# A fused attention and feed-forward kernel: matmuls of 128x128 issued as two of 128x64, some waits left out, the first loads in parts

## The chip, the cores and the metric

The kernel runs on one core of a Trainium2 chip, alone. The metric is the device time of one execution in microseconds (us), taken as the median of several runs. The engines in what follows are PE (TensorE, the matmuls; PEld is its weight loads), DVE (VectorE), ACT (ScalarE), POOL (GpSimd) and SP (SyncE, which issues most of the transfers).

## The reference

Two stages follow each other: an attention whose scores below the row's maximum less `tau` are dropped, and a feed-forward block with ELU. There are 8 sequences of 8 heads, 576 positions and 64 elements, and 4608 tokens of 512 with 2048 hidden units. Everything is computed in f32; the two weight matrices arrive in f64.

```python
scores = scale * np.matmul(q, k.transpose(0, 1, 3, 2))
thresh = np.max(scores, axis=-1, keepdims=True) - tau
scores = np.where(scores >= thresh, scores, -1000000000.0)
...
attn = np.exp(scores - max)
attn = attn / (np.sum(attn, axis=-1, keepdims=True) + 1e-09)
attn_out = np.matmul(attn, v)                  # (8, 8, 576, 64)
x = attn_out.transpose(0, 2, 1, 3).reshape(4608, 512)
h = x @ w_in                                   # (4608, 2048)
g = np.where(h > 0.0, h, np.exp(np.minimum(h, 0.0)) - 1.0)
return g @ w_out                               # (4608, 512)
```

## The kernel before

**Attention.** Heads are taken in 32 pairs, four for a sequence. For a pair the scores come in blocks of 128 queries; head 0 lies in partitions 0 to 63 and head 1 in 64 to 127. A score matmul (`scores`, L494, in the first sequence; `wide_scores`, L769, and the tails at L816 in the others) has 64 rows and 64 columns of weights, so that four of them fill the array. DVE takes the maximum (L518, L776), POOL the threshold (L522, L782), ACT the exponential (L528, L786), DVE drops what lies below the threshold and sums the rest (L538, L790), POOL or ACT divides by the sum (L429, L502), and the block is turned. The first blocks are turned on PE (L555) and copied out of PSUM; the later ones are turned by DVE in squares of 32 (L641), sent to DRAM (L675) and fetched back as `wTa` and `wTb` (L685). The values matmuls follow: `values` (L708 for the 64 tail positions, L713 for the 512 others) in the first sequence, and L821 and L829 later. L713 and L829 hold 64 columns of weights (one head's V), one head in the upper and one in the lower half of the output.

**Feed-forward.** A few chunks are computed plainly: `ffn1` (L888), `ffn1_block` (L916) and `ffn2_plain` (L956), with 128x128 weights. All the others go by seven products of half-size blocks in place of eight: `first_product` (L1447) for x @ w_in, the second round (L1587) for g @ w_out, and in the last stage, when no attention is left, a deeper split of the second (`deep_product`, L1961, 128 columns, and `plain_product`, L2023). Each of these matmuls has 128 rows and 128 columns of weights and 256 or 128 columns that stream through. ACT, DVE and POOL make the sums of the products and the ELU around them.

**The order.** Up to about the ninth pair the order of work is written out by hand: `EARLY` lists some 1270 jobs, each with the engine that does it after a colon, or the PSUM bank after an @. `job(...)` declares what a job needs. Jobs such as `ld.q.0.0` load, `first.k.0.0` turns a piece of the first sequence on PE, `sc.0`, `max`, `exp`, `th`, `mask` and `norm` are the steps of one score block, `half.x` is half a plain feed-forward job, and `idle17` is a run of 17 transposes of the identity, which keep PE going while nothing is loaded. Behind `EARLY` a planner inside the kernel lays the feed-forward jobs between the attention of each pair, by costs and due times, and the deep stage ends the kernel.

**Waits.** The framework derives an instruction's waits from the tiles that it touches. PSUM banks of the wide score tile are handled by the kernel: `on_banks` (called by `watch` and directly) keeps for each bank who touched it and declares every instruction of another engine on these banks as needed.

Of the kernel before, what the change touches and what calls it, by code (L numbers as in the profile page):

```python
# [15 lines left out]
ALU = mybir.AluOpType  # L16
# [4 lines left out]
    "9:3.0": 0.61, "9:fetch0": -3.6, "9:turn4": 2.44, "e:139.1": 0.46, "e:140.2": -0.49, "e:176.2": 1.07,  # L21
    "e:203p0": 1.03, "e:30.2": 0.35, "e:73p0": 1.88, "e:75p0": 1.3, "e:77.2": -1.81, "e:78.1": -3.94, "e:9b":
    -2.29, "e:e30": -0.75,
# [37 lines left out]
ld.tail.1.0 ld.k.0.0:act ld.k.0.1 ld.tau.0.0:act idle17@f0 ld.q.0.0 ld.k.1.1 ld.k.1.0 lw.0 lw.1 first.t.k.0@f0  # L61
ld.k.2.0 tau copy.k.0 first.k.0.0@f2 ld.k.2.1 idle4@f0 prep.k.0.0 ld.k.3.0 first.q.0.0@f0 first.q.1.0@f2 ld.k.3.1
prep.q.0.0 first.t.k.1@f1 sc.0 copy.k.1:dve ld.tail.0.0 lw.2 first.t.k.2@f0 max.0.0 copy.k.2 prep.q.1.0 first.q.2.0@f0
idle7@t max.0.1 exp.0.0 th.0.0 lw.3 first.k.1.0@f2 th.0.1 exp.0.1 mask.0.0 prep.q.2.0 prep.k.1.0 mask.0.1 idle5@f0
first.t.k.3@f1 shift.0 ld.vd.3.0 sc.1 su.0:act copy.k.3:dve sign.0 ld.q.1.0 shift.1 rec.0 rest.0 ld.q.2.0 norm.0.0
first.q.3.0@f0 max.1.0 ld.vd.0.1 prep.q.3.0 first.k.2.0@f0 max.1.1 ld.v.1.1 exp.1.0 th.1.0 rest.1:pool first.t.q.0@f2
ld.q.3.0 part.0.0@t exp.1.1 mask.1.0 th.1.1 first.k.3.0@f1 add.0 prep.k.2.0 mask.1.1 copy.q.0 first.t.q.1@f0 ld.v.0.0
su.1:act sc.2 end.0 norm.0.1:act shift.2 prep.k.3.0 rec.1 part.0.1@f2 norm.1.1 max.2.0 sign.1 idle21@f1 max.2.1
ld.v.0.1 exp.2.0 th.2.0 rest.2:pool ld.vd.0.0 exp.2.1 mask.2.0 th.2.1 add.1 put.0.0 lw.4 mask.2.1 sign.2 rest.3
norm.1.0 sc.3 end.1 ld.v.1.0 su.2:act copy.q.1 put.0.1 add.2 part.0.2@t turn.0 lw.5 max.3.0 part.1.0@f1 put.0.2  # L70
landed.0 ld.vd.2.1 first.q.0.1@f0 max.3.1 exp.3.0 ld.v.3.1 first.q.1.1@f2 th.3.0 rec.2 part.1.1@t th.3.1 exp.3.1
ld.v.2.1 mask.3.0 norm.2.0 ld.vd.1.1 prep.q.0.1 mask.3.1 put.1.1 ld.vd.1.0 part.1.2@f0 turn.1 put.1.0 shift.3 sc.4
end.2 add.3 sign.3 ld.vd.2.0 put.1.2 landed.1 prep.q.1.1 su.3 val.0.block.0@t max.4.0 lw.6 rec.3 max.4.1 exp.4.0
th.4.0 norm.2.1 first.q.2.1@f0 exp.4.1 mask.4.0 part.2.0@f1 th.4.1 norm.3.0 idle7@f2 ld.vd.3.1 norm.3.1:act mask.4.1
ld.v.2.0 put.2.0 end.3 sc.5 su.4:act out.0.block.0 rest.4 shift.4 lw.7 shift.5 sign.4 add.4 ld.v.3.0 part.2.1@t
max.5.0 prep.q.2.1 part.2.2@f1 turn.2 val.1.block.0@f2 max.5.1 exp.5.0 th.5.0 rec.4 th.5.1 exp.5.1 mask.5.0 norm.4.0
part.3.0@f0 put.2.2 put.2.1 landed.2 mask.5.1 part.3.1@f1 norm.4.1 put.3.0 part.3.2@t turn.3 end.4 out.1.block.0
rest.5:pool sc.6 su.5:act put.3.1 sign.5 lw.8 add.5 val.2.block.0@f0 max.6.0 put.3.2 landed.3 rest.6 max.6.1 shift.6
exp.6.0 th.6.0 part.4.0@t rec.5 th.6.1 exp.6.1 mask.6.0 first.q.3.1@f1 add.6 part.4.1@f2 put.4.0 mask.6.1 prep.q.3.1
part.4.2@t turn.4 sign.6 end.5 sc.7 put.4.1 put.4.2:dve landed.4 lw.9 end.6 norm.5.1:act val.3.block.0@t max.7.0  # L80
out.2.block.0 lw.10 norm.5.0:act su.6 max.7.1 th.7.0 exp.7.0 part.5.0@f0 out.3.block.0:dve th.7.1 exp.7.1 mask.7.0
rest.7:pool part.5.1@t part.5.2@f1 turn.5 val.0.block.1@f2 rec.6 mask.7.1 norm.6.1 norm.6.0:act put.5.0 shift.8
rest.8:pool put.5.2 sc.8 su.7 put.5.1 landed.5 rec.7 shift.7 sign.8 add.7 val.1.block.1@t norm.7.0:act max.8.0 max.8.1
exp.8.0 th.8.0 norm.7.1 part.7.0@f0 out.0.block.1:dve out.1.block.1 mask.8.0 exp.8.1 part.6.0@t th.8.1 add.8
part.7.1@f1 put.7.0 mask.8.1 part.6.1@f2 sign.7 part.7.2@f0 turn.7 su.8 sc.9 put.7.1 end.7 rest.9 end.8 lw.11 put.6.1
half.0@f1 shift.9 load.k.4 put.6.0 rec.8 max.9.0 add.9 norm.8.1:act put.7.2:dve landed.7 exp.9.0 max.9.1 part.6.2@t
turn.6 val.3.block.1@f0 th.9.0 norm.8.0:act mask.9.0 th.9.1 lw.12 rest.10:pool exp.9.1 shift.10 sc.10 out.3.block.1
sign.9 add.10 sign.10 part.8.0@f0 put.6.2:dve mask.9.1 landed.6 max.10.0 part.8.1@t su.9:act part.8.2@f2 turn.8 end.9
half.1 exp.10.0 th.10.0 rec.9 put.8.0 put.8.2 lw.13 put.8.1 mask.10.0 norm.9.0 landed.8 end.10 norm.9.1 su.10:act
first.t.q.3@f2 first.t.q.2@f0 sc.11 copy.q.2 copy.q.3 shift.11 rest.11 lw.14 rec.10 val.2.block.1@t fexp.0.0.0  # L90
norm.10.0 max.11.0 max.11.1 exp.11.0 th.11.0 fmin.0.0.0 part.10.0@f0 out.2.block.1:dve exp.11.1 mask.11.0 th.11.1
part.9.0@t add.11 put.10.0 part.9.1@f2 mask.11.1 sign.11 part.10.1@f0 turn.10 shift.12 sc.12 put.10.1 landed.10 end.11
rest.12 shift.13 sign.12 lw.15 add.12 half.4@f0 max.12.0 su.11:act put.9.0 max.12.1 exp.12.0 th.12.0 rec.11 end.12
th.12.1 rest.13 part.9.2@t turn.9 half.5 mask.12.0 exp.12.1 lw.16 add.13 load.q.4 put.9.2 put.9.1 landed.9 mask.12.1
sign.13 sc.13 elu.0.0.0 norm.11.1 su.12 val.0.1@t rec.12 max.13.0 norm.12.0:act norm.12.1 end.13 exp.13.0 th.13.0
fexp.0.1.0 mask.13.0 norm.11.0:act fmin.0.1.0 turn.12 su.13:act rest.14 in.0.0:pool sc.14 rest.15 in.0.1:pool rec.13
send.12 part.11.0@f1 max.14.0 in.0.2:pool half.8@f2 max.14.1 in.1.0:pool exp.14.0 elu.0.1.0 th.14.0 th.14.1 lw.17
out.0.1 put.11.0 shift.15 part.11.1@f0 shift.14 exp.14.1 part.11.2@t turn.11 half.2@f1 add.14 mask.14.0 sign.14
put.11.1 mask.14.1 landed.12 add.15 norm.13.0:act end.14 sc.15 put.11.2:dve landed.11 lw.18 part.13.0@f0 max.15.0
half.3 su.14 max.15.1 exp.15.0 th.15.0 rec.14 sign.15 th.15.1 mask.15.0 exp.15.1 part.13.1@t turn.13 shift.16 sc.16  # L100
rest.16:pool end.15 put.13.0 prep.q.4 add.16 half.9 put.13.1 landed.13 sign.16 mask.15.1 load.q.5 norm.14.1:act
in.1.1:pool max.16.0 su.15:act in.1.2:pool val.1.1@t shift.17 exp.16.0 prep.k.4 th.16.0 fexp.0.0.1 insend.0
in.2.0:pool norm.14.0:act mask.16.0 lw.19 rest.18:pool fmin.0.0.1:act end.16 rest.17 rec.15 shift.18 su.16:act lw.20
sc.17 add.17 out.1.1 rec.16 elu.0.0.1 norm.15.1:act part.14.0@t max.17.1 fexp.0.0.2 norm.15.0 half.6@f0 put.14.0
max.17.0 norm.16.0 fmin.0.0.2:act turn.15 exp.17.0 in.2.1:pool part.14.1@t exp.17.1 th.17.0 part.14.2@f1 turn.14
th.17.1 half.7 send.15 sign.17 add.18 mask.17.0 put.14.2 mask.17.1 in.2.2:pool elu.0.0.2 part.16.0@f1 su.17:act
sign.18 end.17 sc.18 put.16.0 rec.17 end.18 lw.21 norm.17.0:act half.10@f1 max.18.0 put.14.1 landed.14 max.18.1
landed.15 exp.18.0 th.18.0 rest.19:pool in.3.0 lw.22 exp.18.1 half.11 th.18.1 mask.18.0 in.3.1:pool mask.18.1 sc.19
su.18 fexp.0.0.3 in.3.2 rec.18 shift.19 norm.18.0 norm.18.1:act half.14@f2 max.19.0 fexp.0.1.1 scale.4:act turn.18
exp.19.0 th.19.0 rest.20:pool fmin.0.0.3:act part.16.1@t turn.16 half.15 add.19 send.18 put.16.1 landed.16 mask.19.0  # L110
sign.19 in.4.0 fmin.0.1.1:act su.19:act end.19 val.2.1@t fexp.0.1.3 shift.21 lw.23 rest.22 shift.20 rec.19 elu.0.1.1
rest.21 norm.19.0 fmin.0.1.3:act elu.0.0.3 in.4.1:pool norm.17.1:act elu.0.1.3 landed.18 add.21 in.4.2 part.17.0@f0
load.k.5 part.19.0@f1 prep.q.5 put.17.0 part.17.1@f2 add.20 put.19.0 half.18@f0 sign.20 end.20 shift.22 lw.24 out.2.1
put.17.1 sign.21 part.19.1@t turn.19 in.5.0 add.22 part.17.2@f1 turn.17 half.12@f2 put.19.1 landed.19 end.21 put.17.2
landed.17 in.5.1 in.5.2:pool val.3.1@t shift.23 insend.5 sign.23 insend.4 rest.23 lw.25 sign.22 add.23 copy.k.4:act
end.22 prep.k.5 rest.24:pool lw.26 out.3.1 t tail.4 half.19 bmax.4.4.0 insend.2 shift.24 bexp.4.4.0 bth.4.4 add.24
# [60 lines left out]
def kernel(  # L177
# [281 lines left out]
    WBUFS = 3  # L459
    e_both, e_next = att.tile([P, 2, 2, HALF], FP32, name="e", bufs=1), [0]  # L460

    def e_slot():
        e_next[0] ^= 1
        return e_both[:, e_next[0]]

# [1666 lines left out]
```

## Time and profile before

| what | value |
|---|---|
| median of 3 runs (lowest to highest) | 1264.27 us (1262.33 to 1265.05) |
| profiled execution: its time | 1262.88 us |
| profiled execution: its span | 1261.1 us |
| instructions in the span | 24668 |
| DMA | 277.84 MB, 220 GB/s over the span |
| PE records of L1447, L1587, L1961 and L2023 | 1792, 1344, 476, 176 |
| PE records of L829 and L713 (128x64 already) | 896, 192 |

Lines such as L1447 are those of the kernel before. In a group of matmuls `128*128 128x256 f32 x8` reads: weights of 128 rows and 128 columns, a moving operand of 128 partitions by 256 elements, 8 records. An f32 matmul of the program is two records, each with its weight load, while a transpose is one. Records of PE overlap: one of 256 columns lasts about 380 ns in the list, and the next starts long before it ends. So the time that a matmul costs is the distance between starts, and a mean length or a busy share doesn't tell it.

### The profile page before, as it was taken

The numbers are of one execution on the slowest core, as the hardware profiler recorded it, in microseconds if no ns is written. First come the engines' busy times: TensorE is split into PE (matmuls) and PEld (weight loads), VectorE is DVE, ScalarE is ACT, GpSimd is POOL, SyncE is SP. The second block draws the span as 40 slices with busy tenths as digits, with TensorE's granted clock in tenths as the row PEclk, the third lists the DMA queues.
The fourth block names the chain that finished last, engine by engine and source line by source line (L and its number), as shares of the span: only waits on it lengthen the run. The fifth ranks groups of instructions, "written<-read, shape, count | busy, mean of one in ns | idle before, by whom it ended". The sixth has DMA issues, their size and how long they took to land.

```text
span 1261.1 us, 24668 instructions
## 1 busy us (share of the span) xinstructions
PE 1245.4 (99%) x8187; PEld 970.9 (77%) x8187; DVE 1068.6 (85%) x2322; ACT 584.7 (46%) x1276; POOL 788.6 (63%) x1147
## 2 busy tenths in 40 slices
PE   8999999999999999999999999999999999999998
PEld 5776576477777777777788777777777778899998
DVE  6998989898889979898989888988989885777876
ACT  7987755453444435252625353444535260434130
POOL 5775545586576747674767657674757473675554
PEclk9999999999999999999999999999999999999999
DMA  9568898898989898999889898989889876434433
GB/s 225 147 180 240 226 260 244 240 306 213 254 212 262 233 244 223 260 245 237 241 225 268 218 268 202 269 221 251 215 255 248 237 215 219 166 133 150 143 107 112
DMA packets 332880, 277.84 MB, mean 220 GB/s; under 512 B 201296, under 2 KB 288336, under 8 KB 332752
## 3 DMA queue, kind: packets, MB, share of 16 engines
q1 hardware_dynamic: 331760, 275.73, 78.8%
q8 instruction: 65, 1.06, 0.3%
q10 hardware_dynamic: 992, 0.53, 0.1%
q14 instruction: 63, 0.52, 0.1%
HBM read 178.85 MB, written 97.32 MB: 219 GB/s over the span
## 4 chain that ended last, share of the span: by engine, by line
PE 82%; DVE 3%; issue 1%; ACT 0%; DMA 0%; SPq 0%; POOL 0%; DVEq 0%; ACTq 0%
PE f L1447 30%; PE f L1587 23%; PE sc L829 9%; PE sc L769 8%; PE f L1961 4%; PE f L2023 3%; PE sc L821 1%; PE f L888 1%; PE sc L816 1%; DVE mx L776 1%; PE f L956 1%; DVE x L641 1%; DVE e L790 0%; DVE w_one L790 0%; DMA there<-x 0%
## 5 line engine op out<-in xcount | busy, mean ns | idle before, releaser
L776 DVE TENSOR_REDUCE mx<-sc 128x1 f32<-128x576 f32 x252 | 180.2, 746 | 37.8 <-PE sc L769 32.3
L782 POOL TENSOR_SCALAR th<-mx,ntau 128x2 f32<-128x2 f32 (+1 forms) x140 | 46.0, 329 | 187.1 <-DVE mx L776 186.9
L786 ACT ACTIVATE w_one<-sc,mx 128x576 f32<-128x576 f32 x140 | 100.8, 741 | 132.7 <-DVE mx L776 113.3
L790 DVE SCALAR_TENSOR_TENSOR w_one<-sc,th,w_one 128x576 f32<-128x576 f32 x140 | 110.0, 813 | 20.4 <-ACT w_one L786 20.2
L769 PE MATMUL sc<-kT,qT 64*64 64x256 f32 (+5 forms) x1792 | 124.2, 410 | 2.4 <-DVE su L546 0.5
L1447 PE MATMUL f<-xt,sw 128*128 128x256 f32 x512 | 123.8, 384 | 0.6 <-ACT xt L432 0.5
L786 ACT ACTIVATE e<-sc,mx 128x576 f32<-128x576 f32 x112 | 82.8, 743 | 86.6 <-DVE mx L776 85.0
L1447 PE MATMUL f<-x,w_in_sb 128*128 128x256 f32 x512 | 122.8, 382 | 0.0
L1447 PE MATMUL f<-xt,w_in_sb 128*128 128x256 f32 x512 | 121.2, 379 | 0.5 <-DVE xt L1056 0.5
L769 PEld LDWEIGHTS sc<-kT,qT 64*64 64x64 f32 x1792 | 80.7, 132 | 48.3 <-issue 18.2
L502 POOL TENSOR_SCALAR w_one<-w_one,rs 128x576 f32<-128x576 f32 x115 | 89.4, 788 | 38.7 <-DVE rs L552 38.7
L641 DVE STREAM_TRANSPOSE x<-w_one 128x512 f32<-128x512 f32 (+1 forms) x140 | 99.9, 744 | 14.2 <-POOL w_one L502 9.5
L1447 PEld LDWEIGHTS f<-xt,sw 128*128 128x128 f32 x512 | 94.1, 190 | 21.1 <-issue 5.8
L1447 PEld LDWEIGHTS f<-x,w_in_sb 128*128 128x128 f32 x512 | 96.2, 190 | 16.2 <-ACT g L1508 3.6
L1447 PEld LDWEIGHTS f<-xt,w_in_sb 128*128 128x128 f32 x512 | 97.2, 190 | 14.0 <-ACT e L786 0.8
L790 DVE SCALAR_TENSOR_TENSOR e<-sc,th,e 128x576 f32<-128x576 f32 x112 | 87.7, 808 | 8.3 <-ACT e L786 7.9
L1587 PE MATMUL f<-w_out_sb,g 128*128 128x256 f32 x384 | 92.0, 382 | 0.0
L1587 PE MATMUL f<-w_out_sb,s 128*128 128x256 f32 x384 | 91.9, 382 | 0.0
L1587 PE MATMUL f<-t,s 128*128 128x256 f32 x384 | 90.7, 379 | 0.0
L1587 PEld LDWEIGHTS f<-w_out_sb,g 128*128 128x128 f32 x384 | 72.0, 190 | 13.1 <-issue 3.8
L1587 PEld LDWEIGHTS f<-w_out_sb,s 128*128 128x128 f32 x384 | 71.9, 190 | 12.7 <-issue 3.2
L502 POOL TENSOR_SCALAR e<-e,rs 128x576 f32<-128x576 f32 x92 | 67.8, 742 | 20.8 <-DVE rs L552 18.3
(344 smaller groups left out, 2894.1 us busy)
## 6 DMA issues: line engine op xcount, KB each, us to landing
there<-x SPq DMA_DIRECT2D x452, 144.0 KB, 3.8
wTb<-there SPq DMA_DIRECT2D x58, 576.0 KB, 6.4
wTa<-there SPq DMA_DIRECT2D x55, 576.0 KB, 4.7
sw<-win_sums SPq DMA_DIRECT2D x62, 384.0 KB, 4.3
t<-wout_sums SPq DMA_DIRECT2D x45, 512.0 KB, 5.3
there<-x SPq DMA_DIRECT2D x112, 80.0 KB, 1.9
wTb<-there SPq DMA_DIRECT2D x56, 160.0 KB, 3.6
wst<-in_moe_w_in_dram SPq DMA_DIRECT2D x16, 512.0 KB, 4.8
```

The source lines that it names most:

```text
L502: nc.gpsimd.tensor_scalar(wv, wv, st["rs"][:, h : h + 1], 1.0, ALU.mult, ALU.mult)
L641: nc.vector.transpose(x[:, :, c0 : c0 + nc_], src.rearrange("p (c g n) -> p g c n", c=nc_, n=T))
L769: on_banks(nc.tensor.matmul(oy, qT[r, i * P + y * D : i * P + (y + 1) * D], kT[r, k0 : k0 + n], start=True, stop=True, skip_group_check=Tr ...
L776: on_banks(nc.vector.tensor_reduce(st["mx"][:, h : h + 1], st["sc", h], axis=AX.XY if i == NC else AX.X, op=ALU.max, negate=True), st["sc" ...
L782: nc.gpsimd.tensor_scalar(st["th"][:, cs], st["mx"][:, cs], -1.0, ntau, ALU.mult, ALU.add)
L786: on_banks(nc.scalar.activation(st["e", h], st["sc", h], AF.Exp, bias=st["mx"][:, h : h + 1]), st["sc", h])
L790: on_banks(nc.vector.scalar_tensor_tensor(st["e", h], st["sc", h], st["th"][:, h : h + 1], st["e", h], ALU.is_ge, ALU.mult, accum_out=st[" ...
L829: on_banks(nc.tensor.matmul(o, vm[:, h, c], parts[part][:, g0:g1, h * (NC + 1) + c], start=False, stop=(c == NC - 1), skip_group_check=Tru ...
L1447: nc.tensor.matmul(loc["banks"][place], left[:, j], right[:, j], start=(begins and j == 0), stop=(j == 1), skip_group_check=True)
L1587: nc.tensor.matmul(place(m), lhs, rhs, start=(begins and v == 0), stop=(v == RU - 1), skip_group_check=True)
L1961: nc.tensor.matmul(loc["x"][place][:, :P], left[:, v], right[:, v], start=(begins and v == 0), stop=(v == 1), skip_group_check=True)
L2023: nc.tensor.matmul(loc[c][:, :HM], lefts(g, r, c, m)[:, v], rights(r, m)[:, v], start=(v == 0), stop=(v == RU - 1), skip_group_check=True)
```

## The change

- A new helper, `by_columns`, issues a matmul of 128 output rows as two of 64, with the two halves of the weights' columns, the same moving operand and the two halves of the output's partitions. It takes the place of one `nc.tensor.matmul` in `values` (L708), `first_product` (L1447), the second round (L1587), `deep_product` (L1961) and `plain_product` (L2023). `ffn1`, `ffn1_block`, `ffn2_plain` and the transposes stay as they were. The program has 6142 matmuls for 4225.
- `on_banks` passes its list through the new `followed`, which drops a need that another one in the list, or an earlier instruction of the engine, already implies. `exp_of` declares that it needn't wait for the exponential which last wrote its slot.
- The loads of the first 128 queries and of the K tails are made in two parts: heads 0 and 1, then 2 to 7. Each turning job needs only the part that it reads.
- The threshold job may be done by ACT as well as POOL.
- `EARLY` is another order: some 350 of 1270 jobs stand a few places elsewhere, 24 on another engine.

```diff
     def exp_of(pr, i, h):
...
-        on_banks(nc.scalar.activation(e, o, AF.Exp, bias=st["mx"][:, h : h + 1]), o)
+        made = nc.scalar.activation(e, o, AF.Exp, bias=st["mx"][:, h : h + 1])
+        if slot_exps[e_next[0]]:
+            tc.declare_no_dep(made.ins, slot_exps[e_next[0]].name, reason="its mask lies between")
+        slot_exps[e_next[0]] = made.ins
+        on_banks(made, o)
...
-        watch(nc.tensor.matmul(pv[:, :n], vd, wT[:, :, NC], start=True, stop=False, skip_group_check=True), pv[:, :n])
+        by_columns(pv[:, :n], vd, wT[:, :, NC], watch, start=True, stop=False)
...
+    serials, known = {}, {}
+
+    def followed(ins, engine, needed):
+        have = known.setdefault(engine, {})
+        kept_ = []
+        for x in needed:
+            e, n, _ = serials[x.name]
+            if n > have.get(e, -1) and not any(serials[y.name][2].get(e, -1) >= n for y in needed if y is not x and serials[y.name][0] != e):
+                kept_.append(x)
+        for x in kept_:
+            e, n, seen = serials[x.name]
+            for z, m in {**seen, e: n}.items():
+                have[z] = max(have.get(z, -1), m)
+        serials[ins.name] = engine, len(serials), dict(have)
+        return kept_
...
+        needed = followed(ins, engine, needed)
...
+    def by_columns(o, left, right, note=None, **how):
+        n = o.shape[0]
+        for y in range(0, n, D):
+            oy = o[y : y + D] if n > D else o
+            made = nc.tensor.matmul(oy, left[:, y : y + D] if n > D else left, right, skip_group_check=True, **how)
+            if note:
+                note(made, oy)
...
             if what == "q":
-                return w_out_sb[:, NPAIR + z].rearrange("p (h d) -> p h d", d=D), q[0, :, z * P : (z + 1) * P].rearrange("h p d -> p h d")
+                hs = (slice(0, H), slice(0, 2), slice(2, H))[h]
+                return w_out_sb[:, NPAIR + z].rearrange("p (h d) -> p h d", d=D)[:, hs], q[0, hs, z * P : (z + 1) * P].rearrange("h p d -> p h d")
             if what == "tail":
-                return first_tails("qk"[z]), (q, k)[z][0, :, MAIN:].rearrange("h t d -> t h d")
+                hs = (slice(0, H), slice(0, 2), slice(2, H))[h]
+                return first_tails("qk"[z])[:, hs], (q, k)[z][0, hs, MAIN:].rearrange("h t d -> t h d")
...
-                job(("th", n, h), "pool", lambda e, pr=pr, i=i, h=h: bound_of(pr, i, h), ("max", n, h), "tau")
+                job(("th", n, h), "pool|act", lambda e, pr=pr, i=i, h=h: bound_of(pr, i, h, e), ("max", n, h), "tau")
...
                 for j in range(2):
-                    nc.tensor.matmul(loc["banks"][place], left[:, j], right[:, j], start=(begins and j == 0), stop=(j == 1),
-                                     skip_group_check=True)
+                    by_columns(loc["banks"][place], left[:, j], right[:, j], start=(begins and j == 0), stop=(j == 1))
...
-                        nc.tensor.matmul(place(m), lhs, rhs, start=(begins and v == 0), stop=(v == RU - 1),
-                                         skip_group_check=True)
+                        by_columns(place(m), lhs, rhs, start=(begins and v == 0), stop=(v == RU - 1))
...
-                    nc.tensor.matmul(loc["x"][place][:, :P], left[:, v], right[:, v], start=(begins and v == 0), stop=(v == 1),
-                                     skip_group_check=True)
+                    by_columns(loc["x"][place][:, :P], left[:, v], right[:, v], start=(begins and v == 0), stop=(v == 1))
...
-                    nc.tensor.matmul(loc[c][:, :HM], lefts(g, r, c, m)[:, v], rights(r, m)[:, v], start=(v == 0), stop=(v == RU - 1),
-                                     skip_group_check=True)
+                    by_columns(loc[c][:, :HM], lefts(g, r, c, m)[:, v], rights(r, m)[:, v], start=(v == 0), stop=(v == RU - 1))
...
-ld.tail.1.0 ld.k.0.0:act ld.k.0.1 ld.tau.0.0:act idle17@f0 ld.q.0.0 ld.k.1.1 ld.k.1.0 lw.0 lw.1 first.t.k.0@f0
+ld.tail.1.1 ld.k.0.0:act ld.k.0.1 ld.q.0.1:act ld.tau.0.0 ld.tail.1.2:act idle17@f2 ld.q.0.2 ld.k.1.0:act ld.k.3.1
```

More of the change, by code (lines that the diff above doesn't have):

```diff
@@ L86 @@
[L86 to L95, printed above, removed]
@@ L101 @@
[L101 to L105, printed above, removed]
```

229 lines of the change are left out of this document (126 added, 103 removed).

## The prediction

> **What bounds the kernel now.** I read the page first, its busy table and the chain that ended last:
>
> ```profile
> span 1261.1 us, 24668 instructions
> PE 1245.4 (99%) x8187; PEld 970.9 (77%) x8187; DVE 1068.6 (85%) x2322; ACT 584.7 (46%) x1276; POOL 788.6 (63%) x1147
> ...
> PE 82%; DVE 3%; issue 1%; ACT 0%; DMA 0%; SPq 0%; POOL 0%; DVEq 0%; ACTq 0%
> ```
>
> TensorE is busy for 99% of the span and 82% of the chain is its own work, so the end moves only with the PE row. Next, busy time by stage (columns: window, length, then busy us and count of PE, weight loads, DVE, ACT, POOL, granted clock, DMA share, GB/s):
>
> ```profile
> 0.00:63.00 63.00, 56.50 (x550) 42.19 (x550) 50.90 (x121) 53.91 (x112) 38.42 (x72) 1.00 0.72 186
> ...
> 350.00:1117.00 767.00, 766.53 (x4911) 607.39 (x4910) 654.22 (x1413) 325.29 (x721) 494.62 (x732) 1.00 0.84 233
> 1117.00:1262.00 145.00, 140.02 (x878) 129.00 (x876) 107.52 (x243) 33.35 (x86) 81.79 (x98) 1.00 0.39 126
> ```
>
> From 350 to 1117 us PE stands for half a microsecond in all. Waiting is left in the start alone, and the clock is granted in full. In the list of waits, PE's add up to 8.8 us besides the first 1.5 us before anything is loaded, 8.3 of them before 262 us; the longest are:
>
> ```profile
> PE sc L494 <- DVE w L538: 1.4, 4, 0.7
> PE f L555 <- ACT x L426: 1.1, 1, 1.1
> PE sc L816 <- ACT xs L432: 1.1, 1, 1.1
> ```
>
> So two things can pay: a cheaper step of the matmuls, and fewer waits before 262 us. "Busy" doesn't show what a step costs, because the records overlap. That is read from start to start in the timeline (columns: start, length, then the group):
>
> ```profile
> 628.43 1.90 PE L829 MATMUL sc<-wTa,vm 128*64 128x256 f32 x16
> 630.26 2.17 PE L769 MATMUL sc<-kT,qT 64*64 64x448 f32 x32
> 632.36 1.99 PE L1587 MATMUL f<-w_out_sb,g 128*128 128x256 f32 x8
> ...
> 1115.39 1.89 PE L1447 MATMUL f<-x,w_in_sb 128*128 128x256 f32 x8
> 1117.12 1.89 PE L2023 MATMUL f<-w_out_sb,g 128*128 128x256 f32 x8
> ...
> 44.26 1.09 PE L713 MATMUL f<-wTa,vm 128*64 128x128 f32 x16
> 45.28 1.20 PE L494 MATMUL sc<-x 64*64 64x288 f32 x16
> ...
> 1129.00 1.06 PE L1961 MATMUL f<-x,kT 128*128 128x128 f32 x8
> 1129.89 1.89 PE L2023 MATMUL f<-w_out_sb,s 128*128 128x256 f32 x8
> ```
>
> **The step of a matmul in either form.** An f32 matmul leaves two records here. Eight 128x128 records of 256 columns take 1117.12 - 1115.39 = 1.73 us, 216 ns each. The values matmuls (L829) already have the new form, 128x64, and they come in pairs: two records, one in each half of the columns, start 7 ns apart and run side by side. Their 16 records are 8 pairs. From 628.43 to 630.26 are 1.83 us, of which 0.095 us is the change of form at the end (below): (1.83 - 0.10) / 8 = 216 ns a pair. Record by record the means are 215.8 ns for the pair and 215.9 ns for the 128x128 record, so the 1656 matmuls of 256 columns cost the same after as before: 0 us. I bound it at 1 ns on 3312 steps, 3.3 us either way. The weight load behind each is shorter (137 ns for L713's 64 columns, 190 ns at L1447) and hidden in both forms.
>
> **The step at 128 columns** (L1961, in the last stage). Before: (1129.89 - 1129.00) / 8 = 111 ns, 111.6 ns as a mean. L713 is the same shape in the new form: 45.28 - 44.26 = 1.02 us, less 0.095 for the change of form and 0.046 for the first load, over 8 pairs: 109.2 ns. 238 matmuls are 476 steps: 476 x 2.4 ns = -1.1 us. This is the item that I trust least, because the nearest row is only 8 pairs long; see the second rival.
>
> **Entering the form.** A change between 64x64, 128x64 and 128x128 leaves a gap of 91 to 98 ns in the stream at every one of the changes that doesn't also wait, whichever two forms they are. Then the first weight load lies open. Entering 128x128, the row at 632.36 lasts 1.99 us where the undisturbed one has 1.89: 0.10 us (104 ns record by record). Entering 128x64 at L829 it is 46 ns, since the two half loads run together. In the built order the feed-forward matmuls are entered from the score matmuls 46 times, before and after: 46 x (104 - 46) = -2.7 us. I take it whole, since nearly all lie after 262 us, where nothing else holds PE; the bounds are 0 and -2.7. On the way out the second half of a pair starts 7 ns later: 76 exits x 7 ns = +0.5 us.
>
> [...] Counted in the built order, though, changes of form fall from 244 to 237: 12 go at L708 to L713 (the tail's matmul in front of the values takes their form), 5 others come.
>
> 7 x 95 ns is -0.7 us, and 12 first loads of 46 ns at L713 are -0.5 us. They lie before 120 us, where PE waits for ACT and DVE anyway, so I count half: -0.6 us, bounds 0 and -1.2.
>
> **Implied waits left out.** Of instructions that only hold a wait, PE loses 10 of 226 and ACT 67 of 464, while DVE gains 35 on 760. ACT is busy 46%, so its 67 are hidden by its idle time; on DVE one takes 21 ns, 0.7 us over an engine that idles 192 us. A wait that another one implies ends no later than that one, so nothing is released sooner: 0, bounds -0.5 and +0.7.
>
> **First loads in parts, the early order, 24 jobs elsewhere.** The K tails and the first chunk of Q come as heads 0 and 1, then 2 to 7: two issues more, at about 0.5 us each (0.51 us for one on SP at 2.20), three more of them on ACT, which runs its first copy only at 5.68 us. PE's first real matmul starts at 5.28 us, after 17 warm-up transposes which stay; 0.24 us before it are empty, and that is all that an earlier landing gives at once. The next waits (9.46, 11.38 and 14.19 us) are for ACT's copies, not for a load. The threshold on ACT in place of POOL is a 128x1 instruction; the nearest row is ACT's L513 at 0.30 us, against 0.26 us on POOL. The instruction order differs up to some 370 of DVE's 2042 instructions and is the same from there on. What 350 moved jobs do to the 8.3 us of waits no row tells; the work itself is unchanged, and PE, DVE and ACT are busy 56, 51 and 54 of the first 63 us, so not much can be won. I take -1.5 us, with bounds of -8 (all waits gone) and +8 (as much again).
>
> **Sum.** -2.7 + 0.5 - 1.1 - 0.6 - 1.5 + 0 = -5.4 us. The profiled execution took 1262.9 us, 1261.1 of span and 1.8 around it, which gives 1257.5. It was 1.4 us under the median of the runs shown (1264.3), and the runs are what is forecast: 1258.9 us.
>
> **Rivals.** 1. The new early order waits longer (slower). Before 262 us PE stands behind ACT's copies and DVE's masks; if a copy is put behind another, the score matmul waits, then the mask, then the next turn. Nothing later makes it good, since PE has no slack after 350 us. If the 8.3 us double, 1258.9 + 1.5 + 8.3 = 1268.7; it decides from 8 us over my term. Against it: the three engines stay as loaded as before. 2. PE's issue becomes the bound in the last stage (slower). Pairs of 128 columns ask for 4 instructions in 109 ns, 27 ns each, for up to 240 instructions on end (60 matmuls in the built order). For it: nothing in the trace shows that pace for so long. L769 has 64 instructions in 1.87 us, 29 ns each, and the densest long stretch, 33.07 to 50.73 us, has 397 in 17.66 us, 44.5 ns each. If 44.5 ns were the limit, a pair would take 178 ns: 476 x (178 - 111.6) = 31.6 us, so 1258.9 + 1.1 + 31.6 = 1291.6. It decides from 31 ns an instruction (123 ns a pair, +5.4 us). Against it: that stretch is paced by streams of 256 to 320 columns and by changes of form, not by issue. The 256-column pairs need 54 ns and lie within what is shown.
>
> [...]
>
> 3. The form gains nothing: if the half loads follow each other in the feed-forward part, where both halves share one moving operand, the entry costs 104 ns as now and -0.6 - 1.5 - 1.1 + 0.5 = -2.7 is left (1261.6), or -0.6 without the early terms (1263.7): about 1263, no change. L829's 46 ns speak against it, but there the moving operands differ. 4. The early order also removes most waits: 1258.9 - 6 = about 1253.
>
> **How the numbers follow.** Forecast (a gain of 2.5 to 8.5 us) 0.57; rival 4 0.13; rival 3, or the page's 124 ns, 0.13; rival 1 0.10; rival 2 0.07. 0.2% of 1264 us is 2.5 us, about what this measurement can tell from no change: faster 0.70, same 0.13, slower 0.17. The range runs from 1251 (rival 4 with the 3.3 us of the step) to 1268 (most of rival 1); beyond lie rival 2 and the ends of 1 and 4. The forecast's own range is 1255.5 to 1262.
>
> **What would show it.** Right: pairs 7 ns apart with 216 ns from pair to pair at 256 columns and 109 at 128; the first pair after a change of form some 50 ns longer, not 104; some 12,000 PE records (8187 + 2 x 1917); 350 to 1117 us shorter by about 2 us and 1117 to the end by about 1. Wrong: steps of 220 ns or more in long runs, 128-column pairs above 112 ns late in a run (rival 2), or a list of PE's waits before 262 us that isn't near 8 us (rivals 1 and 4).

## The result, and the profile after

| kernel | median of runs (lowest to highest) | ratio to before | profiled span |
|---|---|---|---|
| before | 1263.54 us (1262.33 to 1265.05), 22 runs | | 1261.1 us |
| the changed kernel | 1261.32 us (1258.83 to 1264.81), 22 runs | 0.9983, 95% from 0.9977 to 0.9989 | 1259.3 us |

The changed kernel is 2.2 us faster by the medians, where 5.4 us had been forecast. Its runs spread over 6 us, against under 3 us before. The lines are renumbered: all matmuls of the new form now stand at the helper's line L771, L801 is the score matmul (L769 before), L825 its mask (L790), L864 the values (L829).

The page of the changed kernel shows the same bound:

```profile
span 1259.3 us, 32270 instructions
PE 1242.4 (99%) x12010; PEld 827.7 (66%) x12010; DVE 1066.1 (85%) x2328; ACT 583.7 (46%) x1275; POOL 789.7 (63%) x1142
...
PE 81%; DVE 2%; DMA 2%; SPq 1%; issue 0%; ACT 0%; POOL 0%; DVEq 0%; ACTq 0%; POOLq 0%
```

PE has 12010 records for 8187, and its weight loads shrank from 970.9 to 827.7 us (a median of 137 ns each at L771, for 190 before), which pays nothing at 256 columns, where the step stays at 216 ns (below). New in the chain are DMA and SPq with 3% together: some transfer now has a part in the end. By stage (the windows shown of before):

```profile
0.00:63.00 63.00, 57.28 (x577) 43.38 (x577) 49.73 (x121) 53.63 (x112) 38.49 (x69) 1.00 0.76 189
...
350.00:1117.00 767.00, 766.53 (x7524) 488.71 (x7522) 655.87 (x1418) 326.49 (x725) 496.92 (x735) 1.00 0.84 234
1117.00:1262.00 145.00, 138.37 (x1752) 119.56 (x1748) 107.09 (x242) 33.34 (x86) 81.86 (x98) 0.99 0.38 127
```

The middle is as full as before, with half a microsecond of waits, so what it gains must lie in the steps. PE's work in the timeline of the changed kernel:

```profile
629.44 1.90 PE L864 MATMUL sc<-wTa,vm 128*64 128x256 f32 x16
631.26 2.17 PE L801 MATMUL sc<-kT,qT 64*64 64x448 f32 x32
633.36 1.95 PE L771 MATMUL f<-w_out_sb,g 128*64 128x256 f32 x16
635.14 1.90 PE L771 MATMUL f<-t,g 128*64 128x256 f32 x16
636.87 1.46 PE L771 MATMUL f<-w_out_sb,g 128*64 128x256 f32 x12
...
1118.82 1.04 PE L771 MATMUL f<-x,kT 128*64 128x128 f32 x16
1119.69 1.90 PE L771 MATMUL f<-w_out_sb,g 128*64 128x256 f32 x16
```

From 635.14 to 636.87 are 1.73 us for 8 pairs: 216 ns, as before. The row at 633.36, just behind the change of form, takes 1.78 us: the first pair costs 50 ns more, not 104. From 1118.82 to 1119.69 are 0.87 us for 8 pairs of 128 columns: 109 ns. So the form does what was forecast. The rest is in PE's list of waits, whose longest (behind the 1.5 us before anything is loaded) are

```profile
PE sc L494 <- DVE w L545: 1.9, 4, 0.6
...
PE sc L801 <- DVE w_one L825: 1.3, 2, 0.9
PE f L562 <- ACT x L425: 1.0, 1, 1.0
PE sc L771 <- ACT w_one L425: 0.7, 1, 0.7
```

The list is about as long as before (up to 262 us 8.7 us besides the first row, for 8.3), but the score matmuls' wait for DVE's mask (L769 on L790, 0.3 us before) has become 1.3 (L801 on L825). To see when time is won and lost I compare, between two traces, the starts of the values matmuls of each pair. I call them marks. Differences to the kernel before, in us (negative is earlier):

```
mark near      105    114    171    197    223    286    354   1035   last matmul
after        +2.97  +2.71  +0.73  +2.26  +2.05  +2.07  +1.89  -0.22  -1.68
```

Three things stand here. At 105 us the changed kernel is 3 us late. It has made up 2.2 of them at 171 us and loses some 1.3 again by 286. From there on it gains 3.75 us steadily, at the pace of the form (next run).

### The profile page after: what moved, and what is told of

Read it like the earlier page. It is cut to its first block, busy times and chain, and to the rows that moved or that the text cites. A ratio compares the mean times of both kernels' runs of the same rounds, so it can differ in the third digit from the quotient of the medians.

```text
span 1259.3 us, 32270 instructions
## 1 busy us (share of the span) xinstructions
PE 1242.4 (99%) x12010; PEld 827.7 (66%) x12010; DVE 1066.1 (85%) x2328; ACT 583.7 (46%) x1275; POOL 789.7 (63%) x1142
## 4 chain that ended last, share of the span: by engine, by line
PE 81%; DVE 2%; DMA 2%; SPq 1%; issue 0%; ACT 0%; POOL 0%; DVEq 0%; ACTq 0%; POOLq 0%
PE f L771 60%; PE sc L801 8%; PE sc L864 8%; PE f L991 2%; PE sc L856 1%; PE sc L851 1%; DMA win_sums<-sw 1%; DMA there<-x 1%; DMA wTb<-there 0%; DVE mx L808 0%; DVE x L648 0%; DVE w_one L825 0%; DVE e L825 0%; SPq L354 0%; PE f L923 0%
## 5 line engine op out<-in xcount | busy, mean ns | idle before, releaser
L825 DVE SCALAR_TENSOR_TENSOR w_one<-sc,th,w_one 128x576 f32<-128x576 f32 x140 | 110.0, 812 | 20.3 <-ACT w_one L821 19.1
L801 PE MATMUL sc<-kT,qT 64*64 64x320 f32 (+5 forms) x1792 | 124.2, 410 | 2.4 <-DVE w_one L825 1.3
L771 PE MATMUL f<-xt,sw 128*64 128x256 f32 x1024 | 123.2, 382 | 0.6 <-ACT xt L431 0.5
L771 PE MATMUL f<-x,w_in_sb 128*64 128x256 f32 x1024 | 123.1, 380 | 0.3 <-ACT g L1546 0.3
L771 PE MATMUL f<-xt,w_in_sb 128*64 128x256 f32 x1024 | 121.8, 379 | 0.5 <-DVE xt L1091 0.5
L801 PEld LDWEIGHTS sc<-kT,qT 64*64 64x64 f32 x1792 | 80.9, 132 | 49.5 <-issue 18.5
L771 PE MATMUL f<-w_out_sb,s 128*64 128x256 f32 (+1 forms) x896 | 105.6, 377 | 0.0
L771 PE MATMUL f<-w_out_sb,g 128*64 128x256 f32 (+1 forms) x864 | 101.7, 376 | 0.0
L771 PEld LDWEIGHTS f<-x,w_in_sb 128*64 128x64 f32 x1024 | 74.4, 137 | 37.9 <-ACT g L1546 4.8
L771 PEld LDWEIGHTS f<-xt,w_in_sb 128*64 128x64 f32 x1024 | 75.4, 137 | 35.8 <-ACT e L821 0.9
L771 PEld LDWEIGHTS f<-xt,sw 128*64 128x64 f32 x1024 | 71.9, 137 | 40.9 <-issue 5.0
L825 DVE SCALAR_TENSOR_TENSOR e<-sc,th,e 128x576 f32<-128x576 f32 x112 | 87.7, 806 | 8.3 <-ACT e L821 7.4
L771 PE MATMUL f<-t,s 128*64 128x256 f32 (+1 forms) x800 | 93.5, 375 | 0.0
L771 PEld LDWEIGHTS f<-w_out_sb,s 128*64 128x64 f32 x896 | 63.7, 137 | 31.5 <-issue 3.2
L648 DVE STREAM_TRANSPOSE x<-e 128x640 f32<-128x640 f32 x108 | 77.6, 756 | 5.6 <-POOL e L428 1.7
L771 PEld LDWEIGHTS f<-w_out_sb,g 128*64 128x64 f32 x864 | 61.2, 137 | 31.6 <-issue 3.6
```

What stands on the lines that cost most here:

```text
L648: nc.vector.transpose(x[:, :, c0 : c0 + nc_], src.rearrange("p (c g n) -> p g c n", c=nc_, n=T))
L771: made = nc.tensor.matmul(oy, left[:, y : y + D] if n > D else left, right, skip_group_check=True, **how)
L801: on_banks(nc.tensor.matmul(oy, qT[r, i * P + y * D : i * P + (y + 1) * D], kT[r, k0 : k0 + n], start=True, stop=True, skip_group_check=Tr ...
L825: on_banks(nc.vector.scalar_tensor_tensor(st["e", h], st["sc", h], st["th"][:, h : h + 1], st["e", h], ALU.is_ge, ALU.mult, accum_out=st[" ...
```

## The experiments

Each batch of experiments had its own runs of the kernel before beside it, to which the ratios are taken, with medians of 1263.57, 1263.83, 1263.78 and 1264.16 us.

**The form alone.** The kernel before, with `by_columns` at its five places and nothing else of the change:

```diff
-                    nc.tensor.matmul(loc["banks"][place], left[:, j], right[:, j], start=(begins and j == 0), stop=(j == 1),
-                                     skip_group_check=True)
+                    by_columns(loc["banks"][place], left[:, j], right[:, j], start=(begins and j == 0), stop=(j == 1))
```

> The kernel before with nothing but the new form: by_columns at the same five places; order, loads and waits as before. Theory A (the form gains about 4 us over the whole length, and the new early order gives about 2 of them back before 210 us): 3.5 to 4.5 us faster than before, about 1259.6 us, and PE's waits before 262 us as in the kernel before. Theory B (the form itself gains only about 2 us, the order nothing): about 2 us faster, 1261.5 us.

1259.9 us (12 runs, 1258.53 to 1266.65), ratio 0.9976, from 0.9966 to 0.9986. By the medians the form is worth more alone than the whole change, though the two intervals overlap. Its marks: +0.32 at 286 us, -1.80 at 1035, -3.12 at the last matmul. So nothing is won before 286 us, and 3.44 us behind it.

**The rest without the form.** The changed kernel with `by_columns` issuing one 128x128 matmul again:

```diff
-        for y in range(0, n, D):
-            oy = o[y : y + D] if n > D else o
-            made = nc.tensor.matmul(oy, left[:, y : y + D] if n > D else left, right, skip_group_check=True, **how)
+        made = nc.tensor.matmul(o, left, right, skip_group_check=True, **how)
```

> The changed kernel with 128x128 matmuls again; order, loads in parts and left-out waits stay. Theory A: 1.5 to 3 us slower than before, about 1265.5 us, because what is left of the change is the early order, which waits longer. Theory B: as before, within 1 us.

1263.98 us (11 runs), ratio 1.0001, from 0.9993 to 1.001. The median is nearer to the second theory; the trace shows 1.79 us lost at 286 us, of which 1.22 are left at the last matmul. The interval (from -0.9 to +1.3 us) leaves room for both.

**The order undone.** The changed kernel with the old `EARLY`, in which each split load is two jobs:

```diff
-ld.tail.1.1 ld.k.0.0:act ld.k.0.1 ld.q.0.1:act ld.tau.0.0 ld.tail.1.2:act idle17@f2 ld.q.0.2 ld.k.1.0:act ld.k.3.1
+ld.tail.1.1 ld.tail.1.2 ld.k.0.0:act ld.k.0.1 ld.tau.0.0:act idle17@f0 ld.q.0.1 ld.q.0.2 ld.k.1.1 ld.k.1.0 lw.0 lw.1
```

> The changed kernel with the early order of before (each load that is now in two parts stands as two jobs where the whole one stood). Theory A: about 2 us faster than the changed kernel, near 1259.5 us, with less spread from run to run. Theory B: as the changed kernel, 1261.3 us.

1259.49 us (5 runs), ratio 0.9961, from 0.9949 to 0.9973. Beside the changed kernel's 0.9983 this is the first theory's result, and the two intervals don't overlap: the early order costs about 2 us (1.8 by the medians, 2.8 by the ratios).

**The waits undone.** The changed kernel without `followed` and without the exponential's declaration:

```diff
-        needed = followed(ins, engine, needed)
...
-        if slot_exps[e_next[0]]:
-            tc.declare_no_dep(made.ins, slot_exps[e_next[0]].name, reason="its mask lies between")
-        slot_exps[e_next[0]] = made.ins
```

> The changed kernel without followed and without the declaration in exp_of, so with all implied waits. If an implied wait costs nothing: as the changed kernel, within 0.5 us of 1261.3. If the 50 instructions that ACT is spared matter: 1 us slower or more.

1260.91 us (10 runs, 1259.79 to 1262.10), ratio 0.9975, from 0.9967 to 0.9984. Putting the implied waits back costs nothing that these runs can tell.

**Where in the order.** Two kernels with half of either order, joined at the job `main.4.1` (about 171 us). First the old order up to it and the new one behind it:

> The changed kernel, its early list put together from two: the order of before up to the values of the fifth pair (main.4.1, about 171 us), the new order for what is left. In the traces so far the kernels with the new order are level at 171 us and 1.3 to 1.9 us later by 286 us. Theory A (the loss is made behind 171 us): near the changed kernel, 1261 us. Theory B (the first part, below 171 us, sets up the loss): near the kernel with the old order throughout, 1259.5 us.

1262.55 us (11 runs, 1259.44 to 1266.22), ratio 0.9988, from 0.9979 to 0.9997. Then the new order up to it and the old one behind it:

> The other way round: the new order up to main.4.1, the order of before for what is left. Theory A: near 1259.5 us or below, as with the old order throughout. Theory B: near the changed kernel, 1261 us.

1259.04 us (5 runs), ratio 0.9962, from 0.9948 to 0.9975. So the loss lies behind 171 us. The marks agree: from 171 to 286 us the new order loses 1.3 us (the changed kernel) and 3.6 us (old, then new), the old one gains 0.9 (new, then old).

**How the halves pair.** The form alone, but `first_product` issues the two accumulating matmuls of the upper half of the output and then those of the lower half:

```diff
-                for j in range(2):
-                    by_columns(loc["banks"][place], left[:, j], right[:, j], start=(begins and j == 0), stop=(j == 1))
+                for y in (0, D):
+                    for j in range(2):
+                        nc.tensor.matmul(o[y : y + D], left[:, j, y : y + D], right[:, j], start=(begins and j == 0), stop=(j == 1),
+                                         skip_group_check=True)
```

> The kernel with the form alone (e1), in which first_product issues the two matmuls of the upper half and then the two of the lower half, not upper and lower in turn. Theory A (PE starts its records in program order, so halves run side by side only when they are neighbours): of 8 records only one of each four finds a partner, 6 steps in place of 4, so the 387 us of first_product get 50% longer, about 1450 us in all. Theory B (PE picks the other half out of its queue): as e1, 1260 us.

1262.58 us in its single run. Two rows of `first_product` in its timeline:

```profile
682.98 1.95 PE L1457 MATMUL f<-xt,w_in_sb 128*64 128x256 f32 x16
684.70 2.05 PE L1457 MATMUL f<-x,w_in_sb 128*64 128x256 f32 x16
```

From one to the next are 1.72 us for 8 pairs, which is the step of the second theory: the halves run side by side and the steps stay at 216 ns, though the second half now starts some 58 ns behind the first and not 7. How PE comes to start them so isn't shown. A single run 2.7 us above the form alone lies within that kernel's spread. 1.6 us of the difference are seen in PE's waits of this kernel, the rest isn't accounted for:

```profile
PE f L1457 <- DMA sw<-win_sums: 1.6, 2, 1.0
```

PE waits for the feed-forward's sums, which are fetched back from DRAM one block ahead. In the trace of the kernel before this wait doesn't occur.

**Is issue near a bound?** The form alone in quarters of 32 columns, four instructions where there was one:

```diff
-        for y in range(0, n, D):
-            oy = o[y : y + D] if n > D else o
+        for y in range(0, n, T):
+            oy = o[y : y + T]
```

> The kernel with the form alone (e1), in quarters of 32 columns in place of halves. It doubles the instructions once more: 27 ns for each in the steps of 256 columns, 14 ns in those of 128. Theory A (PE issues one instruction in about 27 ns at best): the 256-column steps stay near 216 ns, the 476 steps of 128 columns go from 109 to about 216 ns, 1310 us in all. Theory B (issue is far from a bound): 109 ns stay, and the first load after a change of form falls to some 25 ns from 46; 1259 us. Theory C (an instruction needs some 40 ns in the long run): also the 256-column steps grow, to 320 ns, over 1550 us.

1267.46 us in its single run. Two stretches of its timeline:

```profile
689.62 3.37 PE L747 MATMUL f<-xt,sw 128*32 128x256 f32 x32 [2.49 <-DMA sw<-win_sums]
692.82 1.04 PE L747 MATMUL f<-x,sw 128*32 128x256 f32 x16
693.68 1.90 PE L747 MATMUL f<-xt,w_in_sb 128*32 128x256 f32 x32
...
1133.98 1.06 PE L747 MATMUL f<-x,kT 128*32 128x128 f32 x32
1134.85 1.91 PE L747 MATMUL f<-w_out_sb,s 128*32 128x256 f32 x32
```

The row at 1133.98 has 32 matmul records and 32 weight loads in 0.87 us: 13.6 ns an instruction, and eight steps of 109 ns. The longest stretches at 128 columns, 240 matmul records on end, keep nearly that pace: 27.1 and 27.6 ns a record, each with its weight load. So issue isn't the limit at 27 ns an instruction either, and the theory that put it there falls. The other half of theory B holds too: behind a change of form the first step takes 240 ns, 24 more than the next ones, where two halves take 267. The loss is elsewhere: 3.7 us of waits for `sw`, and what the first row shows. Behind its pause of 2.5 us, 32 records take 3.2 us in place of 1.73. The windows of that kernel say why (columns: window, length, PE busy and count, granted clock, DMA share, GB/s):

```profile
685.76:689.17 3.41, 1.37 (x24) 1.00 0.95 313
689.17:692.59 3.42, 2.97 (x28) 0.50 0.96 308
```

For 3.41 us the granted clock is a half, which costs 1.7 us. With the waits for `sw` that makes 5.4 of the 7.6 us over the form alone; the rest isn't accounted for. More on the clock below.

**Which part behind 171 us.** Two more joints, the second at `main.5.1` (about 197 us): new, old between 171 and 197, new again; and new up to 197 us, then old.

> The new order up to main.4.1 (about 171 us) and again from main.5.1 (about 197 us), the old one between. Theory A: what the new order loses arises between these two jobs, where the eighth pair's scores come to wait for a mask on DVE; then this kernel ends as the one with the old order in all that follows 171 us, near 1259.0 us, and its trace holds no wait of 0.9 us of the scores for DVE's mask near 203 us. Theory B: the loss comes from the jobs after 197 us, which meet DVE's queue in the same state whatever lies before; then about 1261.3, as the changed kernel.

1259.83 us (6 runs), ratio 0.9968, from 0.9955 to 0.998.

> The new order up to main.5.1 (about 197 us), then the old one. Theory A (the loss arises between 171 and 197 us): about 1261.3 us, as the changed kernel, with 2 us lost against the kernel that goes over to the old order at 171 us by 286 us. Theory B (it arises after 197 us): about 1259.0.

1260.29 us (7 runs), ratio 0.9974, from 0.9963 to 0.9985. Neither theory's picture: from 171 to 286 us either trace loses about half a microsecond (0.44 and 0.60), where the five with the new order in all of that stretch lose 1.3 to 3.9. The medians lie in between too, but the intervals overlap with those on both sides, so these runs don't tell how the loss is shared. But the last trace taught something that wasn't asked. Up to 171 us it has the very order of the kernel that is new, old, new, and yet it is 2.4 us late at 105 us, like the changed kernel. Followed instruction by instruction, the two part on POOL, in a step of the conversion of the weights. The changed kernel shows the same step, POOL's timeline first, then SP's:

```profile
86.36 0.44 POOL L525 TENSOR_SCALAR th<-mx,ntau 128x1 f32<-128x1 f32 x1
89.79 0.91 POOL L284 TENSOR_SCALAR wst<-wst 128x512 f32<-128x512 uint32 x1 [2.99 <-DMA wst<-in_moe_w_out_dram]
```

```profile
78.93 0.38 SPq L1047 DMA_DIRECT2D win_sums<-w_out_sb  x1
80.50 0.33 SPq L272 DMA_DIRECT2D wst<-in_moe_w_out_dram  x1
```

POOL waits 3.0 us for a 512 KB weight piece. The new order sends 384 KB of sums to DRAM 1.6 us ahead of that load. The kernel before has it the other way round:

```profile
79.97 0.33 SPq L273 DMA_DIRECT2D wst<-in_moe_w_out_dram  x1
86.93 0.50 SPq L1012 DMA_DIRECT2D win_sums<-w_out_sb  x1
```

Behind POOL's step stand its part of the next normalisation and threshold, so ACT, DVE and in the end PE's matmuls come late.

**That one job put back.** In the changed kernel the sending of the sums goes behind two more loads of weight pieces (parts of the lines of `EARLY`):

```diff
-landed.11 insend.0 lw.18
+landed.11 lw.18
...
-rest.18:pool in.2.0:pool
+rest.18:pool insend.0 in.2.0:pool
```

> The changed kernel with one job of the early order, the sending of the first 384 KB of the feed-forward's sums to DRAM (win_sums), put back behind two more loads, as in the order before. In the profile of the changed kernel this write is issued at 78.93 us, 1.6 us ahead of a load of a weight piece that POOL then waits 3.0 us for; in two other kernels of the same order the piece was in time. Theory A: the write ahead of the load is what makes the piece late, in some runs and not in others. Then POOL has no such wait, the values matmuls near 105 us start 2 to 3 us sooner than in the profile of the changed kernel, the median falls by about 1 us, to about 1260.3, and the runs spread less than the 6 us of the changed kernel. Theory B: the load is late whatever is ahead of it (the score loads behind it do it): the wait stays in some runs, median 1261.3, spread 6 us.

1261.53 us (11 runs, 1259.95 to 1262.19), ratio 0.9977, from 0.9968 to 0.9986. The median hasn't moved. The instructions on `wst` between 70 and 95 us, in the changed kernel and then in this one:

```profile
DMA to landing us min/median/max: 4.7/5.2/9.1
```

```profile
DMA to landing us min/median/max: 4.7/4.9/5.3
```

POOL has no such wait here, and the mark at 105 us is at +0.10 for +2.97. One trace can't show that the wait never comes, since four of six traces with the write ahead of the load have no such wait either. But the load itself tells more. Of the pieces asked for near 80 us, the one behind the write landed after 6.1 to 9.1 us in all six traces with the write 1.3 to 1.7 us ahead of it, and after 4.3 to 5.0 us in seven of the eight without (6.1 in the eighth, the last kernel below). So the piece is later with the write ahead, by 1 to 2 us in four traces and by some 4 in two; why, and what held it up in the eighth, stays open. The spread proves nothing for it: it is 2.2 us here and 6 in the changed kernel, but also 2.3 with the waits undone, which has the changed kernel's order, and 8.1 with the form alone, which has the old one.

The lead is at -1.47 us at 171 and gone at 286 (+2.41). PE's timeline of this kernel, then DVE's:

```profile
199.35 1.90 PE L866 MATMUL sc<-wTa,vm 128*64 128x256 f32 x16
202.97 3.14 PE L803 MATMUL sc<-kT,qT 64*64 64x448 f32 x32 [1.73 <-DVE w_one L827]
206.04 2.94 PE L993 MATMUL f<-w_out_sb,g 128*128 128x512 f32 x4
208.82 1.89 PE L925 MATMUL f<-xt,w_in_sb 128*128 128x256 f32 x8
```

```profile
189.00 1.44 DVE L650 STREAM_TRANSPOSE x<-e 128x640 f32<-128x640 f32 x2 [0.77 <-DMA there<-x]
190.36 0.72 DVE L810 TENSOR_REDUCE mx<-sc 128x1 f32<-128x576 f32 x1
...
200.68 1.44 DVE L650 STREAM_TRANSPOSE x<-e 128x640 f32<-128x640 f32 x2 [1.32 <-ACT g L911]
202.04 0.78 DVE L827 SCALAR_TENSOR_TENSOR w_one<-sc,th,w_one 128x576 f32<-128x576 f32 x1
```

PE's score matmuls wait 1.7 us for the mask (L827), and the mask stands behind a turn (L650) that waits 1.3 us. Its place in DVE's queue isn't the cause: the old order has the same two turns ahead of the same mask. DVE's timeline of the last kernel below, which has the old order here:

```profile
196.42 1.44 DVE L650 STREAM_TRANSPOSE x<-w_one 128x640 f32<-128x640 f32 x2
197.78 1.41 DVE L650 STREAM_TRANSPOSE x<-e 128x640 f32<-128x640 f32 x2
199.11 0.77 DVE L827 SCALAR_TENSOR_TENSOR w_one<-sc,th,w_one 128x576 f32<-128x576 f32 x1
```

There no turn waits. What the turn waits for here is most likely its buffer, which a transfer to DRAM (`there<-x`) still reads, as in the row at 189.00. The row at 200.68 names ACT, but the six traces with the new order between 171 and 197 us name four different instructions of it. In all six this turn waits (0.5 to 1.9 us) and starts 0.18 us behind the landing of a `there<-x`, here at 200.50; in the eight with the old order these transfers have landed 1.4 us or more before it, and it doesn't wait. They are late on SP's queue, first in this kernel, then in the last one:

```profile
191.10 5.69 SPq L684 DMA_DIRECT2D there<-x  x8
```

```profile
188.85 4.56 SPq L684 DMA_DIRECT2D there<-x  x8
```

Ahead of them the new order issues three fetches (`wTa`, `wTb`), a 384 KB write of sums and four more `there<-x`, which land 6.2 to 7.2 us later; the old one issues the write some 5 us earlier, ahead of the fetches. Which of these moves does it wasn't tried. Then the clock, in the windows:

```profile
201.18:204.60 3.42, 1.64 (x24) 1.00 0.88 168
204.60:208.01 3.41, 3.41 (x19) 0.50 0.96 266
```

PE was busy for 48% of one window of 3.41 us, and in the next its clock is a half, which costs another 1.7 us: the score matmuls take 3.14 us and not the 2.46 of the next kernel's row, and the four records behind them 2.94 and not 1.98. Three of this kernel's 11 runs have a mean clock of 0.998, as its trace has, and they are among its four slowest.

**Both repaired.** The same job put back in the kernel with the new order up to 171 us and the old one behind it:

> The same one job put back in the kernel that has the new order up to main.4.1 and the old one behind it. Theory A: no run meets the late piece; the two losses of the new order are both gone, about 1258.5 us, the lowest of all, with runs within 2 us. Theory B: as that kernel, 1259.0 us or more, with single runs 2 us above.

1256.96 us (5 runs, 1256.30 to 1258.25), ratio 0.9947, from 0.9935 to 0.996. This is the fastest of all, 6.6 to 7.2 us under the kernel before and 4.4 under the changed one by the medians, and 1.5 under what the first theory gave. That the one job is worth anything here isn't separated by the intervals (0.9962 without it, up to 0.9975). PE in the same place:

```profile
197.69 1.90 PE L866 MATMUL sc<-wTa,vm 128*64 128x256 f32 x16
200.06 2.46 PE L803 MATMUL sc<-kT,qT 64*64 64x448 f32 x32 [0.47 <-ACT xt L433]
202.45 1.98 PE L993 MATMUL f<-w_out_sb,g 128*128 128x512 f32 x4
```

The wait is 0.47 us and nothing of the clock is lost.

The marks of the traces side by side show both places (differences to the kernel before, in us). Each row is one run: the changed kernel and the same with its waits undone have one order and end 1.7 us apart, so the marks tell where time goes and the medians how much:

```
mark near             105    171    197    223    286   1035   last matmul
form undone         +0.40  -0.08  +0.69  +1.11  +1.79  +1.50  +1.22
form alone          +0.36  +0.29  +0.29  +0.30  +0.32  -1.80  -3.12
order undone        -0.05  -0.27  -0.28  -0.59  +0.02  -1.85  -3.32
waits undone        +0.06  -1.15  -0.07  +0.44  +0.64  -1.84  -3.41
changed kernel      +2.97  +0.73  +2.26  +2.05  +2.07  -0.22  -1.68
new, old, new       -0.08  -1.57  -1.58  -1.80  -1.13  -2.96  -4.42
new to 197, old     +2.33  +0.84  +0.83  +1.13  +1.44  +0.39  -1.14
old, then new       +0.20  -0.02  +0.57  +3.28  +3.62  +1.36  +0.11
new, then old       -0.09  -1.46  -1.47  -1.63  -2.33  -3.06  -4.48
sums sent later     +0.10  -1.47  -0.30  +1.99  +2.41  +1.01  -0.55
both repaired       -0.33  -1.95  -1.96  -2.27  -2.35  -4.05  -5.57
```

## Why the prediction was right, and where it was wrong

The time of 1261.3 us lies in the range, and in the forecast's own (1255.5 to 1262). The latter is luck: the kernel before came out 0.7 us faster over 22 runs than over the three known then, and from those the same gain would have led to 1262.1. The gain of 2.2 us lies under the 2.5 to 8.5 that the forecast stood for, and under the 0.2% that it took for what can be told from no change, though the interval of the ratio leaves 1 out.

**The form: right in kind and nearly in size.** Forecast were -2.7 (entries), +0.5 (exits), -1.1 (the step at 128 columns) and -0.6 (fewer changes of form, fewer open loads before 120 us), in sum -3.9. The form alone gave 3.1 us in its trace and 3.7 by the medians. The signs of each row were seen: 50 ns at the entry, 109 ns at 128 columns, 216 ns at 256 columns in either form. Only the -0.6 before 120 us never came: that trace is 0.36 us late at 105 us, and PE's waits up to 120 us are 0.6 us longer than before. Nothing of it should have been counted where the forecast itself said that PE waits. The stages came out too, in the changed kernel's trace: 354 to 1035 us shortened by 2.1 us (about 2 forecast from 350 to 1117) and the rest by 1.5 (about 1 from 1117).

**The implied waits: right.** Zero was forecast, and putting them back showed no loss.

**The early order: the step that failed.** "I take -1.5 us, with bounds of -8 (all waits gone) and +8 (as much again)." It cost about 2 us: the kernel with the old order is at 0.9961 of the time before, for 0.9983, and in the traces the changed kernel stands at +2.07 us at 286 us where the form alone stands at +0.32. This one term is some 3.5 us off, about the whole miss of 3.2. The bounds held it, so the range did; the value within them had nothing behind it but the hope that moved jobs move waits the right way. That the loss lies behind 171 us was shown by undoing the order there. The traces show two places. Ahead of 105 us a weight piece is late behind the sums sent to DRAM, which cost 2 to 3 us in two of six traces; that moving the one job gains time wasn't shown by the medians. Near 200 us a turn on DVE waits, by its timing for a late transfer, and the mask and the score matmuls behind it wait too; this is read from the traces, and only the whole stretch around it was undone. Both are places in SP's queue, which the forecast didn't read: it looked at PE, DVE and ACT and found them as loaded as before. The first 171 us of the new order are, in five of six traces in which the piece is in time, 1.2 to 2.0 us better than the kernel before, which is the size forecast; what follows gives it back. The forecast's own sign for such a loss, waits of PE before 262 us that aren't near 8 us, didn't show it: they come to 8.7.

**Rival 1 (the early order waits longer)** came nearest: a turn, a mask and the score matmuls late one behind the other. But its first link was to be a copy on ACT, and by the traces it was a transfer. It decides from 8 us over the term, as the forecast had it; the runs show 3.5.

**Rival 2 (issue in the last stage) and its 44.5 ns** fall with the quarters: 13.6 ns an instruction over one row, and nearly that over 240 records on end. The 124 ns a pair that stand beside rival 3's chance are shown by no run: the 128-column pairs took 109 ns, and so did the steps of four quarters.

**Rival 3 (the half loads follow each other)** falls with the 50 ns at the entry, in kernels where both halves share one moving operand. **Rival 4** (most waits vanish) didn't happen in the changed kernel, and even the kernel with both places repaired ends at 1257.0, not at the 1253 worked out for it.

**What stays open.** How the loss behind 171 us is shared between the jobs up to 197 us and those behind, and which job makes the transfers late there. Why the weight piece is late by so much in two of six traces. What makes the runs of one kernel spread: the slowest runs of the form alone, the form undone and old, then new (1266.2 to 1266.8 us) have a mean clock of 0.997 or 0.998, but the slowest of the changed kernel (1264.81) has 1.000. And what is next: PE waits for the sums fetched from DRAM (`sw`) in seven of the thirteen traces other than that of the kernel before, from 0.2 to 3.7 us, but not in the fastest, and a remedy wasn't tried.

## What to carry to other kernels

A gain in the form of a matmul is worked out from starts in the timeline, and here that came within 1 us (3.9 us forecast, 3.1 in the trace and 3.7 by the medians); a rearranged order is a change of its own and wants its own experiment, since here it ate about half of what the form gave. Before moving a job, look at the queue that it is moved in: a transfer put ahead of another that an engine needs soon, or a step that waits for a transfer put ahead of one that PE needs, can cost more than the job (here 3.0 us on POOL in the changed kernel's trace, and 1.7 on PE in that with the sums sent later). A wait that names another instruction in every trace is better looked for among the transfers that landed just before its end (here 0.18 us before it, in six traces). Where runs of one kernel spread, compare two traces of the same order instruction by instruction: the first place where they part shows the wait.

## What the runs showed of the hardware

**A half clock for 3.41 us behind a pause of 1.7 to 2.5 us.** In three traces (the sums sent later, the quarters, and old, then new) the granted clock was 0.50 for 3.41 us in the middle of the kernel, each time behind 3.41 us in which PE was busy for 48%, 40% and 32%; the pauses were of 1.73, 2.49 and 2.31 us. A stretch of 3.41 us with PE busy for 56% (the kernel with the form undone, pause of 1.5 us) left the clock as it was: the mean over that trace is 1.000. The stretch of 32% and the one behind it, in old, then new, and the stretch of 56%:

```profile
202.00:205.41 3.41, 1.10 (x18) 1.00 0.86 160
205.41:208.83 3.42, 3.42 (x26) 0.50 0.98 262
...
200.90:204.31 3.41, 1.90 (x22) 1.00 0.83 136
```

In the traces of the kernel before and of the changed one the full clock is granted for 1256.105 and 1252.691 us on end, which are 368 and 367 times 3.413 us. From these lengths and the three half stretches of 3.41 us I estimate that the clock is granted anew every 3.413 us, so that the place of a pause of 1.7 us among these steps would decide whether it costs another 1.7 us. No run moved such a pause alone to show it.

**Halves pair by themselves.** Two matmuls in different halves of the columns run side by side even when two matmuls of one half are issued first: steps of 216 ns in either order (1.73 and 1.72 us for 8 pairs). **A weight piece lands later behind a write.** 512 KB asked for near 80 us landed after 6.1 to 9.1 us in the six traces with 384 KB sent to DRAM 1.3 to 1.7 us ahead, and after 4.3 to 5.0 in seven of the eight others (6.1 in one).
